# Long convolution and spectral mix on one core: earlier W reads, ten Z rooms, and the identity behind the last pair

## The chip, the cores and the metric

The kernel runs on one core of one Trainium2 chip. The metric is the time of one execution in device microseconds; lower is better. Engines are named as the profile names them: PE (matmuls), PEld (its weight loads), DVE, ACT, POOL and SP. POOL and SP also issue DMAs: POOL's go to the queue that the profile calls q0 software_dynamic, SP's to q1 hardware_dynamic. Both queues are served by the same 16 DMA engines.

## What is computed

`x` is 8 x 5696 x 128, `h` is 5696 x 128, and there are 64 modes with complex 128 x 128 matrices. Cut to what matters:

```python
L = 2 * S                                   # causal convolution along the sequence
y = irfft(rfft(x, L) * rfft(h, L), L)[:, :S]
X = rfft(y)[:, :64]                         # spectral mix of the first 64 modes
Yr = einsum(Xr, w_r) - einsum(Xi, w_i)
Yi = einsum(Xr, w_i) + einsum(Xi, w_r)
u = y + irfft(Yr + 1j * Yi, n=S)
out = u + relu(u @ w_ch)
```

## The kernel before

The eight batches go through in four pairs (`NP = 4`). The work has three parts.

*First transforms* (`a_tile`, 32 tiles per pair): a transform of the input over 89 rows, into the tile `As`.

*Frequency ticks* (`tick(g_, t)` for each pair `g_`, 23 pieces `s = 0 .. 22` and three ticks of lag): a second transform from `As` with the constants `M` into PSUM (`second`), ACT's copy of it to `Xs`, DVE's product with the transformed filter `Hs` (`products`, into `U`), two matmuls with `Wc`, and two evictions by ACT into a *Z room*, a 128 x 1024 tile. From the room PE reads the piece for the low modes (constants `G`, one tick later), and a DMA on SP's queue writes it to the scratch tensor `zscr` in HBM (512 rows of 512 bytes; half of that for piece 22). A room is free for its next piece when both have happened. Rooms 0 to 5 are called `Zs` in the profile, 6 to 9 `Zt`. Between two pairs the next pair's first transforms run (L700), and the pieces of w_r and w_i are rewritten to the scratch tensor `wscr`.

*The tail* (from L710): the mix of the 64 modes with `W` (2 x 64 matrices, read back from `wscr` into `W` in four DMAs of 1 MB), eviction of the result to `Y` (L780), eight transposes of `Y` on PE with the identity `Id` as moving operand (L785), eviction to `C`, and then 16 chunks of 16 sequence columns: each is read from `zscr` into `ZT0` to `ZT4` in turn (a DMA of 128 rows of 8 KB and one of 52 rows), transformed back with `S4a` and `S4b`, joined with the mix's part (`C`, `IBs`), evicted to `UT`, and multiplied by `w_ch` (`WI`); ACT's relu and DVE's addition make the output tile, which SP's queue writes out. A part of chunk 0's matmuls is done between the parts of the mix.

Each engine has one list of instructions, in the order in which the program adds them; `Recorder` adds the waits that reads and writes of named tokens require. `after=` adds a wait for all that wrote or read a token before. A DMA takes its semaphore from a ring, and waits for the ring's earlier user of that semaphore.

What the change touches:

- `NZS` (L230): the rooms per pair, 6, 10, 10 and 8. With 8 in the last pair, rooms 8 and 9 are not used in it; the tile `Y` and the identity lie in their memory (`r_off`, L274). `ZY` names the tokens of these two rooms, `ZX` those of rooms 6 and 7.
- the ring "z" of the writes to `zscr` (L293), with 8 semaphores.
- `early` (L529): what the last pair starts at which tick, on POOL's queue: the identity at 0, W's pieces at 1, 3, 6 and 8, `S4b` at 12, the clearing of `ZT0b` at 14, `ZT0` at 15, `S4a` at 16, and at 21 `IBs`, `ZT1` and `ZT2`. `pace` makes each wait for the tick's `U`.
- `SLACK` (L535): `ZT1` waits until the last pair's pieces 0 to 14 have landed in `zscr`. `ZT3` and `ZT4` follow after the loop (L711 to L714), all in POOL's one queue.
- `load_w` (L483): each piece waits for all writes of `wscr`; piece 0 also for all reads of the input tile `Xin`, in whose memory `W` lies.

Of the kernel before, what the change touches and what calls it, by code (L numbers as in the profile page):

```python
# [4 lines left out]
P = 128  # L5
# [118 lines left out]
def bass_long_conv_fft__then__afno_spectral_mix_kernel(nc, x, h, moe_w_r, moe_w_i, moe_w_ch, out):  # L124
# [8 lines left out]
    NP = B // 2  # L133
    KT = 4
    NT = (NK + KT - 1) // KT
# [15 lines left out]
    c, s = np.cos(th), np.sin(th)  # L151
# [35 lines left out]
    def const(name, a):  # L187
        return nc.inline_tensor(np.ascontiguousarray(a.astype(np.float16)), name=name)
# [3 lines left out]
    c_w = const("cW", np.concatenate([w1, w2, np.eye(P)], axis=1))  # L192
# [5 lines left out]
    zs = nc.dram_tensor("zscr", [NP * NK * P, 2 * D], F16, kind="Internal")  # L198
# [7 lines left out]
    def at(name, cols, dt, off):  # L206
        return nc.alloc_sbuf_tensor_at(name, [P, cols], dt, offset=off)

    def take(nbytes):
        off = (cur[0] + 31) // 32 * 32  # L210
        cur[0] = off + nbytes
        assert cur[0] <= end, (cur[0], end)
        return off
# [13 lines left out]
    g_sb = at("G", GW, F16, a_g)  # L227
    ah_sb = at("Ah", HW, F16, a_g)
    NU, NXS, NZ, NZX = 3, 2, 6, 10
    NZS = [NZ] + [NZX] * (NP - 2) + [8]  # L230
    NZL = NZS[-1]
    a_st = take((2 * NU + NXS + NZ) * 2048)
    h_in = at("Hin", J * D, F16, a_st)
    DH = D // 2
# [45 lines left out]
    id_sb = at("Id", P, F16, r_off[1])  # L280
# [8 lines left out]
    def pv(bank, off, dims, p0=0, n=P):  # L289
        return bass.AP(ps, p0 * 4096 + bank * 512 + off, [[4096, n]] + [list(d) for d in dims])  # L290

    R = Recorder(nc)
    for name, n in (("c", 16), ("x", 26), ("z", 8), ("w", 16), ("t", 10), ("s", 8), ("o", 12), ("p", 16), ("q", 10)):  # L293
        R.ring(name, n)

    def bank(i):
        return ("bank", i)
# [3 lines left out]
    def evac(dst, src, reads, writes, scale=None, eng=None, after=()):  # L301
        e = eng
        if e is None:
            turn[0] ^= 1
            e = "scalar" if turn[0] else "vector"
        if e == "scalar":
            if scale is None:
                R.add(e, lambda h_: h_.copy(dst, src), reads, writes, after=after)  # L308
            else:
                R.add(e, lambda h_: h_.activation(dst, src, COPY, scale=scale), reads, writes, after=after)  # L310
        elif scale is None:
            R.add(e, lambda h_: h_.tensor_copy(dst, src), reads, writes, after=after)  # L312
        else:
            R.add(e, lambda h_: h_.tensor_scalar_mul(dst, src, scale), reads, writes, after=after)  # L314

    def dma(eng, dst, src, ring, reads=(), writes=(), after=()):
        R.add(eng, lambda h_: h_.dma_start(dst, src), reads, writes, ring=ring, after=after)  # L317
# [6 lines left out]
    def once(key, toks):  # L324
        if key in first:
            return []
        first[key] = 1
        return list(toks)
# [3 lines left out]
    def turns(name, items):  # L332
        i = ring2.get(name, 0)
        ring2[name] = i + 1
        return items[i % len(items)]
# [87 lines left out]
    for j in range(16):  # L423
        t = turns("h", [0, 2, 4])
# [11 lines left out]
        if j % 2:  # L436
            i = j // 2 % 2 * XC + j // 4
# [45 lines left out]
    def load_w(i):  # L483
        w = 2 * M * D // 4
        dma("gpsimd", w_sb[:, i * w:(i + 1) * w], bass.AP(wd, i * w, [[2 * M * D, P], [1, w]]),
            "p", WD, [("w", i)] + (XIN if i == 0 else []), after=pace)
# [4 lines left out]
    M_ALL = [("m", i) for i in range(MP)]  # L491
    G_ALL = [("g", i) for i in range(NG)]
    WT = [("w", i) for i in range(4)]
    ZY = [("zs", i, b) for i in range(NZL, NZX) for b in range(2)]
    ZX = [("zs", i, b) for i in range(NZ, NZL) for b in range(2)]
    zt_old = [(AST, AST), (AST, AST), (H_ALL, H_ALL), (H_ALL, H_ALL), (M_ALL[3:6], G_ALL)]

    def load_zt(i, eng="sync", more=()):
        g_, c_ = divmod(i, J // ZB)
        for part, (p0, r0, n) in enumerate(((0, 0, P), (PB, P, RB))):  # L500
            old = list(once(("zt", i % NC, part), zt_old[i % NC][part])) + list(more) + pace
            dma(eng, bass.AP(zt[i % NC][part], p0 * ZP, [[ZP, n], [1, ZP]]),
                bass.AP(zs, (g_ * 2 * NK + r0) * J * 256 + c_ * ZB * 256, [[J * 256, n], [1, ZP]]),
                "q" if eng == "gpsimd" else "t", [("zd", g_, s_) for s_ in range(NT)], [("zt", i % NC, part)], after=old)

    def clear_zt(i):
        z32 = zt[i][1][0:PB, :].bitcast(U32)
        R.add("gpsimd", lambda e: e.memset(z32, 0), (), [("zt0", i)], after=list(zt_old[i][1]) + pace)

    def load_ib():  # L510
        dma("gpsimd", ib_sb[:, 0:SH], c_ib.ap(), "p", (), [("ib", 0)], after=M_ALL[0:2] + pace)
# [10 lines left out]
    def load_s4(part):  # L522
        n = PB + RB if part else P
        dma("gpsimd", s4_sb[part][0:n, 0:SH], bass.AP(c_s4, part * SH, [[2 * SH, n], [1, SH]]), "p", (),
            [("s4", part, 0)], after=pace + (AST if part else M_ALL[1:4]))

    V, A = "vector", "scalar"
    border = {NT - 1: [(0, 0, V)], NT: [(1, 2, V), (2, 0, V)], NT + 1: [(3, 2, A), (4, 0, V)], NT + 2: [(5, 2, V)]}
    early = {0: lambda: load_id(), 1: lambda: load_w(0), 3: lambda: load_w(1), 6: lambda: load_w(2), 8: lambda: load_w(3),  # L529
             12: lambda: load_s4(1), 16: lambda: load_s4(0),  # L530
             14: lambda: clear_zt(0),
             15: lambda: load_zt(0, "gpsimd"),
             NT - 2: lambda: (load_ib(), load_zt(1, "gpsimd", SLACK), load_zt(2, "gpsimd"), clear_zt(1), clear_zt(2))}
    pace = []
    SLACK = [("zd", NP - 1, s_) for s_ in range(NT - NZL)]  # L535

    def load_id():
        dma("gpsimd", id_sb[:, :], bass.AP(c_w, 2 * P, [[3 * P, P], [1, P]]), "p", (), [("id",)], after=ZY)

    def load_wi():  # L540
        dma("gpsimd", wi_sb[:, P:2 * P], bass.AP(c_w, 2 * P, [[3 * P, P], [1, P]]), "p", (), [("i16",)], after=M_ALL[5:6])
# [2 lines left out]
    def keep(n, b0):  # L544
        for i in range(n):
            mm(pv(b0 + i % 2, 0, [[1, 2 * NK]]), f1_sb[:, 0:P], f1_sb[:, :], True, True, [("f1",)], [bank(b0 + i % 2)])
# [66 lines left out]
    def zroom(g_, s_):  # L613
        return (s_ - 2 * NZ) % NZX if g_ == 0 and s_ >= 2 * NZ else s_ % NZS[g_]

# [69 lines left out]
            filter_tick((j - 11) // 3, [h_, h_ + 1])  # L685
    keep(16, turns("s", FOUR))
    for g_ in range(NP):
        for t in range(NT + LM):
            tick(g_, t)
            if g_ == 0 and t < 2:  # L690
                keep(8, 4)
            assert g_ + 1 < NP or not wp
            if g_ == NP - 1 and t in early:
                pace[:] = [("u", min(t, NT - 1) % NU)]
                early[t]()
        evac(bass.AP(xt, 2 * g_ * XTW + M, [[B * XTW, P], [XTW, 2], [1, P]]), pv(MB, 0, [[P, 2], [1, P]]),
             [bank(MB)], [("xt", g_)], 1.0 / 64, eng="scalar", after=[("ag", k) for k in range(NS + 2 * XN, NK)])
        evac(bass.AP(xt, 2 * g_ * XTW, [[B * XTW, P], [XTW, 2], [1, M]]), pv(MB, M, [[P, 2], [1, M]]),
             [bank(MB)], [("xtn", g_)], -1.0 / 64, eng="vector" if g_ + 1 == NP else "scalar", after=[("ag", k) for k in range(NS + 2 * XN, NK)])
        if g_ + 1 < NP:  # L700
            for j in range(6, 32):
                a_tile(j, [(4, 6, 0, 2)[(j - 7) % 4] if j > 6 else 0], "both" if j == 31 else V if j % 2 else A)
                if j == 31:
                    keep(8, 6)
                if wp and j % 2 == 1:
                    dst, src_, ring, tok = wp.pop(0)
                    dma("gpsimd", dst, src_, ring, (), [tok], after=[("as", j)])
# [71 lines left out]
    for hb in range(2):  # L779
        evac(bass.AP(y_sb, hb * 32 * B, [[2 * M * B, P], [B, 32], [M * B, 2], [1, B]]),  # L780
             pv(6 + hb, 0, [[2 * B, 32], [B, 2], [1, B]]), [bank(6 + hb)], [("y", hb)], eng="vector" if hb else "scalar",
             after=ZY)
    for b in range(B):
        bk = 6 + b // 4
        R.add("tensor", lambda e, b=b, bk=bk: e.transpose(  # L785
# [10 lines left out]
    o_cur = [0]  # L796
    o8_old = [H_ALL] * 2 + [U_ALL] + [G_ALL + ZX] * 2 + [WT] * 2
    o_old = [H_ALL] * 2 + [M_ALL[5:6], U_ALL + [("f1",)]]
# [49 lines left out]
    for g_ in range(NP):  # L848
        last = g_ == NP - 1
        order = [(c_, b) for b in range(2) for c_ in range(NCH)] if last else [(c_, b) for c_ in range(NCH) for b in range(2)]  # L850
        for n, (c_, b) in enumerate(order):
            i = NCH * g_ + c_
# [44 lines left out]
```

## Time and profile before

| | |
|---|---|
| median of 3 runs | 393.89 us (393.86 to 394.1) |
| the profiled execution | 392.87 us, of which span 390.6 us |
| PE busy | 364.1 us, 93% of the span |
| DVE, ACT, POOL busy | 301.9 us, 311.2 us, 85.6 us |
| DMA | 103.94 MB, mean 266 GB/s |
| ticks of the last pair | about 221 to 263 us |
| mix, transposes, first UT eviction | 264 to 273 us |
| chunks and output | to the end |

A profile line of a group gives line, engine, operation, tile written and tiles read, and a count. A wait line says who waited for whom, the total, how often, and the longest. The chain is the work that ended last, followed back from the end. A DMA's time to landing runs from its issue to the update of its semaphore. All times within the execution are counted from the span's start.

### The profile page before, as it was taken

What the parts mean: (1) busy time and instruction counts of PE and PEld (TensorE: products, weight loads), DVE (VectorE), ACT (ScalarE), POOL (GpSimd) and SP (SyncE); (2) the same over time, 40 slices, a digit from 0 to 9 for tenths busy, and PEclk for the clock granted to TensorE, in tenths of its full rate; (3) what the DMA queues carried; (4) which work ended last, traced back from release to release, by engine and by line L of the source; (5) the groups of instructions that cost most, each with busy time, mean ns of one, the idle gap of its engine ahead of it and who ended that gap; (6) DMA issues with size and microseconds to landing.
All of it is one profiled execution on the core that took longest, in us unless ns stands there. A gap on an engine that the chain in (4) does not pass through costs nothing.

```text
span 390.6 us, 12485 instructions
## 1 busy us (share of the span) xinstructions
PE 364.1 (93%) x5346; PEld 281.3 (72%) x5346; DVE 301.9 (77%) x346; ACT 311.2 (80%) x489; POOL 85.6 (22%) x134
## 2 busy tenths in 40 slices
PE   7799899998989999999989899989989999999992
PEld 7698766665866667856657666658878988988871
DVE  3369889987998998989998988754437767677784
ACT  8289689997989997899997899984447676777783
POOL 8600022210643210823213210319200000000000
PEclk9899999999999999999999999996999999999998
DMA  7998569998899995999995689999999999998766
GB/s 146 178 283 337 138 126 297 274 251 251 92 135 201 238 268 169 127 136 231 245 261 111 64 264 351 298 354 379 406 388 393 414 407 412 410 399 356 305 274 273
DMA packets 87090, 103.94 MB, mean 266 GB/s; under 512 B 22824, under 2 KB 72616, under 8 KB 83564
## 3 DMA queue, kind: packets, MB, share of 16 engines
q1 hardware_dynamic: 62523, 67.73, 49.7%
q0 software_dynamic: 24512, 35.43, 43.6%
q8 instruction: 42, 0.69, 0.7%
q14 instruction: 13, 0.10, 0.1%
HBM read 70.61 MB, written 51.12 MB: 312 GB/s over the span
## 4 chain that ended last, share of the span: by engine, by line
PE 63%; DMA 15%; DVE 8%; ACT 6%; issue 3%; POOL 3%; SPq 0%; POOLq 0%; DVEq 0%
PE ps L320 63%; DMA ZT4b<-zscr 4%; DMA zscr<-Zt 3%; DMA Hs<-Hs 3%; DMA Hin<-in_h_dram 3%; DMA Xt<-in_x_dram 2%; DVE As L314 2%; DVE U L599 2%; ACT As L310 2%; DVE U L607 1%; DVE Xin L361 1%; ACT UT L308 1%; ACT Zs L308 1%; DVE Hs L312 1%; ACT Xs L308 1%
## 5 line engine op out<-in xcount | busy, mean ns | idle before, releaser
L607 DVE TENSOR_TENSOR U<-Xs,Hs 128x2048 f16<-128x2048 f16 (+1 forms) x73 | 86.9, 1192 | 15.1 <-ACT Xs L308 11.0
L320 PE MATMUL ps<-U,Wc 128*128 128x512 f16 (+1 forms) x368 | 94.0, 376 | 1.3 <-DVE U L607 0.8
L308 ACT CAST Xs<-ps 128x1024 f16<-128x1024 f32 (+1 forms) x77 | 74.7, 974 | 11.9 <-PE ps L320 6.8
L308 ACT CAST Zs<-ps 128x512 f16<-128x512 f32 (+1 forms) x134 | 70.6, 595 | 2.7 <-PE ps L320 2.4
L832 DVE TENSOR_TENSOR O<-ps,R 128x512 f32<-128x512 f32 x81 | 52.5, 685 | 19.8 <-ACT R L831 12.5
L831 ACT ACTIVATE R<-ps 128x512 f32<-128x512 f32 x96 | 50.9, 572 | 16.3 <-PE ps L320 15.8
L314 DVE TENSOR_SCALAR As<-ps 128x720 f16<-128x720 f32 x70 | 57.7, 884 | 5.4 <-PE ps L320 4.8
L320 PE MATMUL ps<-F,Xin 128*128 128x180 f16 x512 | 53.7, 249 | 3.6 <-DVE Xin L361 2.3
L320 PE MATMUL ps<-As,M 64*128 64x128 f16 x1440 | 50.5, 217 | 3.5 <-DVE U L599 2.9
L320 PEld LDWEIGHTS ps<-F,Xin 128*128 128x128 f16 x512 | 44.4, 155 | 12.1 <-DVE Xin L361 2.8
L320 PE MATMUL ps<-WI,UT 128*128 128x256 f16 x360 | 51.8, 279 | 0.5 <-DVE O L832 0.4
L320 PEld LDWEIGHTS ps<-U,Wc 128*128 128x128 f16 x368 | 28.7, 97 | 30.3 <-ACT Zs L308 4.4
L310 ACT ACTIVATE As<-ps 128x720 f16<-128x720 f32 (+1 forms) x61 | 45.7, 770 | 5.7 <-PE ps L320 4.3
L317 POOL DMA_DIRECT2D Xt<-in_x_dram x48 | 26.0, 546 | 101.0 <-PE ps L320 97.1
L320 PEld LDWEIGHTS ps<-As,M 64*128 64x128 f16 x1440 | 40.6, 94 | 9.9 <-DVE U L599 3.6
L308 ACT CAST UT<-ps 128x712 f16<-128x712 f32 x40 | 30.0, 752 | 18.7 <-PE ps L320 17.7
L320 PEld LDWEIGHTS ps<-WI,UT 128*128 128x128 f16 x360 | 39.3, 152 | 4.2 <-issue 1.9
L320 PE MATMUL ps<-IBs,C 128*128 128x356 f16 x128 | 40.5, 326 | 0.6
L320 PEld LDWEIGHTS ps<-G,Zs 128*128 128x128 f16 x524 | 26.6, 96 | 14.9 <-ACT Zs L308 2.2
L607 DVE TENSOR_TENSOR U<-ps,Hs 128x2048 f16<-128x2048 f32 x15 | 34.3, 2283 | 0.0
L320 PE MATMUL ps<-G,Zs 128*128 128x128 f16 (+2 forms) x524 | 33.0, 192 | 0.1
L312 DVE CAST UT<-ps 128x712 f16<-128x712 f32 x24 | 21.4, 890 | 11.0 <-PE ps L320 11.0
(87 smaller groups left out, 509.8 us busy)
## 6 DMA issues: line engine op xcount, KB each, us to landing
out_dram<-O SPq DMA_DIRECT2D x39, 512.0 KB, 8.7
zscr<-Zs SPq DMA_DIRECT2D x64, 256.0 KB, 7.4
Xt<-in_x_dram POOLq DMA_DIRECT2D x24, 320.0 KB, 7.3
zscr<-Zt SPq DMA_DIRECT2D x24, 256.0 KB, 7.3
W<-wscr POOLq DMA_DIRECT2D x4, 1024.0 KB, 9.1
M<-cM POOLq DMA_DIRECT2D x5, 720.0 KB, 20.6
ZT0a<-zscr SPq DMA_DIRECT2D x3, 1024.0 KB, 13.1
Hs<-Hs SPq DMA_DIRECT2D x44, 64.0 KB, 6.3
```

What stands on the lines that cost most here:

```text
L308: R.add(e, lambda h_: h_.copy(dst, src), reads, writes, after=after)
L310: R.add(e, lambda h_: h_.activation(dst, src, COPY, scale=scale), reads, writes, after=after)
L312: R.add(e, lambda h_: h_.tensor_copy(dst, src), reads, writes, after=after)
L314: R.add(e, lambda h_: h_.tensor_scalar_mul(dst, src, scale), reads, writes, after=after)
L317: R.add(eng, lambda h_: h_.dma_start(dst, src), reads, writes, ring=ring, after=after)
L320: R.add("tensor", lambda h_: h_.matmul(o, l, r, start=st, stop=sp), reads, writes)
L361: R.add("vector", lambda e: e.tensor_copy(bass.AP(x_sb, i * XN * XS, [[XW, NQ], [XS, XN], [1, D]]), src), list(toks) + XZ, [("xin", i)])
L599: R.add("vector", lambda e, b=b, s_=s_: e.tensor_tensor(bass.AP(u_s[i], b * 512, [[2048, P], [1024, 2], [1, n * D]]), s_, hv, MULT), [tok, ...
L607: R.add("vector", lambda e: e.tensor_tensor(uv, src, hv, MULT), bk + [("h", t, 0), ("h", t, 1, 0), ("h", t, 1, J)], [("u", i)])
L831: R.add("scalar", lambda e: e.activation(rv, src_r, RELU), bk, [("r", i % NR)], after=once(("r", i % NR), G_ALL + XTT + [("y", 0), ("y", 1 ...
L832: R.add("vector", lambda e: e.tensor_tensor(ov, src_u, rv, ADD), bk + [("r", i % NR)], [key + (h_,)], after=once(key, old))
```

## The change

```diff
-    NZS = [NZ] + [NZX] * (NP - 2) + [8]
-    NZL = NZS[-1]
+    NZS = [NZ] + [NZX] * (NP - 1)
...
-    for name, n in (("c", 16), ("x", 26), ("z", 8), ("w", 16), ...
+    for name, n in (("c", 16), ("x", 26), ("z", 10), ("w", 16), ...
...
-    ZY = [("zs", i, b) for i in range(NZL, NZX) for b in range(2)]
-    ZX = [("zs", i, b) for i in range(NZ, NZL) for b in range(2)]
+    ZX = [("zs", i, b) for i in range(NZ, NZX) for b in range(2)]
...
-    early = {0: lambda: load_id(), 1: lambda: load_w(0), 3: lambda: load_w(1), 6: lambda: load_w(2), 8: lambda: load_w(3),
-             12: lambda: load_s4(1), 16: lambda: load_s4(0),
+    early = {3: lambda: load_w(2), 6: lambda: load_w(3), 10: lambda: load_s4(1), 16: lambda: load_s4(0),
              14: lambda: clear_zt(0),
              15: lambda: load_zt(0, "gpsimd"),
-             NT - 2: lambda: (load_ib(), load_zt(1, "gpsimd", SLACK), load_zt(2, "gpsimd"), clear_zt(1), clear_zt(2))}
+             18: lambda: load_ib(),
+             NT - 2: lambda: (load_zt(1, "gpsimd", SLACK), load_zt(2, "gpsimd"), clear_zt(1), clear_zt(2)),
+             NT + 2: lambda: load_id()}
     pace = []
-    SLACK = [("zd", NP - 1, s_) for s_ in range(NT - NZL)]
+    SLACK = [("zd", NP - 1, s_) for s_ in range(NT - 8)]
 
     def load_id():
-        dma("gpsimd", id_sb[:, :], bass.AP(c_w, 2 * P, [[3 * P, P], [1, P]]), "p", (), [("id",)], after=ZY)
+        dma("sync", id_sb[:, :], bass.AP(c_w, 2 * P, [[3 * P, P], [1, P]]), "c", (), [("id",)], after=ZX)
...
     for g_ in range(NP):
+        if g_ == NP - 1:
+            load_w(0)
+            load_w(1)
         for t in range(NT + LM):
...
         evac(bass.AP(y_sb, hb * 32 * B, [[2 * M * B, P], [B, 32], [M * B, 2], [1, B]]),
              pv(6 + hb, 0, [[2 * B, 32], [B, 2], [1, B]]), [bank(6 + hb)], [("y", hb)], eng="vector" if hb else "scalar",
-             after=ZY)
+             after=ZX)
```

`NT` is 23. `SLACK` covers the same pieces 0 to 14 as before. `ZX` now names rooms 6 to 9, all of which the last pair uses: the identity's load and both evictions to `Y` wait for what was last read from them. The identity's load is SP's last issue of the pair, behind the write of piece 22. `W`'s pieces 0 and 1 are issued by POOL ahead of the last pair's first tick, without a pace. Apart from the two rooms more, the instructions on PE, ACT and DVE and their order stay as they were; the lines behind the edit in `NZS` move up by one and those behind the two new calls down.

More of the change, by code (lines that the diff above doesn't have):

```diff
@@ L292, in bass_long_conv_fft__then__afno_spectral_mix_kernel @@
     R = Recorder(nc)
-    for name, n in (("c", 16), ("x", 26), ("z", 8), ("w", 16), ("t", 10), ("s", 8), ("o", 12), ("p", 16), ("q", 10)):
+    for name, n in (("c", 16), ("x", 26), ("z", 10), ("w", 16), ("t", 10), ("s", 8), ("o", 12), ("p", 16), ("q", 10)):
         R.ring(name, n)
```

## The prediction

> **What bounds the kernel now.** I read the page first: PE is busy 93% of the span, so a gain or a loss is time in which PE waits. Next the waits by pair between 215 and 300 us, where the last pair runs and the tail begins:
>
> ```profile
> POOL ZT1a L317 <- DMA zscr<-Zt: 2.4, 1, 2.4
> ACT Zt L308 <- DMA zscr<-Zt: 1.0, 1, 1.0
> PE ps L320 <- DMA ZT4b<-zscr: 1.8, 1, 1.8
> ```
>
> Columns: who waited for whom, total, times, longest. ACT stands 1.0 us before the last Z piece (s = 22) because room Zt0 still holds s = 14, whose write to zscr has not landed. PE stands 1.8 us before chunk 4. The chain that ended last ties the two (start, us, what):
>
> ```profile
> 250.16 11.91 DMA zscr<-Zt
> ...
> 262.59 0.53 POOL ZT1a L317
> ...
> 273.48 15.12 DMA ZT4b<-zscr
> 288.59 0.05 issue
> 288.64 11.36 PE ps L320 x163
> ```
>
> Piece 14's write, issued at 250.16, takes 11.91 us. ZT1a waits for it (SLACK), everything behind ZT1a on POOL's queue follows, and ZT4b lands at 288.59. Between 288 and 391 us the waits name PE, ACT and DVE among each other and no DMA but that ZT4b, so the tail is paced by the engines: what PE loses before it is added to the end.
>
> Third, the identity's tile, the eight transposes that need it, and its load:
>
> ```profile
> L785 PE MATMUL ps<-Id,Y x8: 302/311/311, 269.8 to 270.6; 128*128 128x128 f16 x8
> L317 POOL DMA_DIRECT2D Id<-cW x1: 569/569/569, 216.4 to 216.4; - x1
> ```
>
> The load is issued 53 us ahead. The transposes stand in PE's one queue: while they wait, all that follows waits.
>
> Fourth, the queue to which the load moves. SP's last issue of the pair and its time to landing, and both DMA queues between 268 and 272 us (packets, MB, share):
>
> ```profile
> 264.31 1.89 SPq L317 DMA_DIRECT2D zscr<-Zt  x1
> ```
> ```profile
> zscr<-Zt SPq DMA_DIRECT2D x1, 128.0 KB, 20.1
> ```
> ```profile
> q0 software_dynamic: 236, 1.43, 88.3%
> q1 hardware_dynamic: 263, 0.13, 11.0%
> ```
>
> The smallest write of all takes 20.1 us, from 264.31 to 284.4. The last fence shows why: POOL's queue (q0, rows of 8 KB) and SP's (q1, rows of 512 B) get one packet each in turn, so SP moves an eleventh of the bytes as long as POOL's ZT loads last.
>
> **W pieces 0 and 1 ahead of the pair.** In the trace they are issued at 225.28 and 228.43. They need the last first transforms (PE is through them at 219.9) and the last write of wscr, which lands at 220.7 (issued at 215.71, 5.0 us). So they go at about 221. No PE wait is named after W: piece 3, the last, is issued at 236.75, takes 9.2 us, and is first used at 264.4. Directly this earns 0. Indirectly it lets 2 MB go while DMA is idle: from 215 to 225 us it moves 60 GB/s and nothing after 221. The start is 4.5 us earlier, and piece 14 (5 us behind its queue now) meets less: it may land between 254 and 262 in place of 262.07. Then ZT1a is held by the pace of tick 21 alone, which let the IB load go at 259.62 in this trace: ZT1a goes between 259.7 and 262.6, a gain of 0 to 2.9 us for the ZT stream. S4b's and IB's earlier ticks move the same bytes; nothing waits for either in the trace: 0. But IB, 128 packets, leaves a stretch (259 to 264 us) in which SP sent 2160 packets and POOL 123; in its new place, about 254.4 (three ticks of 1.75 us ahead), it runs right behind S4a and leaves the writes of pieces 15 to 19 later than now.
>
> **Ten rooms and a ring of ten.** Piece 22 takes room 2 of piece 12, whose write has landed by 253.0. ACT's 1.0 us goes, if PE's next need is not later anyway. The old ring of eight is not named in any wait: 0.
>
> **The identity behind SP's queue.** One DMA of 32 KB, 128 packets of 256 B, so 8 on each of 16 engines; SP's issue costs some 0.4 us of an idle sequencer. It is issued after piece 22's write (so not before 263), waits until the writes of pieces 16 to 19 (rooms Zt0 to Zt3) have landed, and its packets stand behind those of pieces 20, 21 and 22: 32+32+16 per engine. Landings of SP's queue are in order throughout the trace (273.5, 280.4, 284.4 for these three). Both Y evictions get the same wait for pieces 16 to 19, and the transposes need Y as well.
>
> The price: the ZT stream has 45 packets of 8 KB per engine (four chunks of 128+52 rows, over 16) and 16 small ones of WI. At 1.43 MB in 4 us (268 to 272) the stream's 5.9 MB take 16.5 us, or 0.27 us for each of an engine's 61 packets. In that time SP gets about as many turns, 61, fewer than the 80 packets ahead of the identity. So the identity lands no sooner than POOL's stream runs dry. The nearest row says the same: piece 22 landed 21.8 us after ZT1a's issue. With ZT1a at 259.7 to 262.6 this is 281.5 to 284.4; the identity's own 8 packets and its wait for piece 19, later than now through IB, add 0.5 to 3. I take 285.0, near the upper end because of that wait; bounds 281 to 288. Nothing covers it: the 16 matmuls and the eviction that precede the transposes are done by 269.8, and ACT, DVE and POOL have nothing that feeds PE.
>
> **The sum.** Transposes at 285.0 in place of 269.84: +15.2. From there PE needs the 17 us of work it has now before chunk 4; that chunk has long landed by 302, so its wait of 1.8 goes. ACT's 1.0 us lies ahead of the new stall and earns 0; without the stall it would count. Sum +13.4 us. The profiled execution is 390.6 us of span and 392.87 in all; it becomes 404.0 and 406.3. The median of the runs is 393.89, 1.0 above, so 407.3.
>
> The clock: granted 0.82 in 263 to 270 and 0.56 in 270 to 275, 1.00 before and after, so the transposes already meet a slow PE. [...] My sum takes the cost as equal on both sides, since the trace shows 4.5 us at the low rate after 269.84 now; bounds -0.6 and +1.2.
>
> **Rivals.**
> 1. *SP's queue is served in bigger bites.* If SP gets several packets per turn, pieces 20 to 22 and the identity pass during the first two chunks: ZT2b landed 15 us after ZT1a's issue (277.6), so with ZT1a at 259.7 to 262.6 the identity lands at 274.7 to 277.6, say 276: +6.2-1.8, so 398.3. For it: 2160 packets of SP in 5 us when POOL has little. Against: 236 against 263 with both full. [...]
> 2. *The identity is in time.* If the earlier W empties the queues so far that pieces 16 to 22 land by 266, the identity is there at about 268.8, and both old waits go: -1.0-1.8, so 391.1. It decides below a landing of 271.6 (269.84 plus 1.8 given back); past that the change costs. For it: the queues hold up to 1.6 MB less by 250 (4.5 us at 0.36 MB/us). Against: pieces 20 to 22 are evicted between 259.3 and 262 however empty the queues are, ZT1a follows by 262.6 at the latest, and in that company their writes took 11.4, 17.6 and 20.1 us.
> 3. *It doesn't reach the end.* The identity lands at about 271.6, so that the stall only takes the place of the waits given back: 393.9. Against: the same three writes; and a longer stall isn't made up later, since PE is busy 39.6 of 40 us from 310 to 350.
>
> **Chances.** Forecast 0.82, rival 1 0.10, rival 2 0.06, rival 3 0.02. A measurement tells this kernel from no change at about 0.2%, 0.8 us. Faster 0.06, same 0.02, slower 0.92. Range: identity at 281 to 288 and the clock's bounds give 402.7 to 411.5; I widen it to 401 to 412 towards rival 1.
>
> **What would show it.** Right: one PE wait of 12 to 18 us before L787 (the transposes' new line), ended by the DMA of Id; Id issued on SP after 263 and landing near 285; W's first two loads at about 221; no ACT wait for room Zt0; no PE wait before chunk 4; the tail from the transposes to the end as long as now less 1.8 us. Wrong: Id landing before 272, a PE wait there under 2 us, or a tail that shortens by more than the clock's 1.2 us.

## The result and the profile after

| | before | changed |
|---|---|---|
| median of 6 runs | 393.14 us (388.19 to 394.1) | 404.66 us (402.09 to 407.3) |
| ratio to the kernel before | 1 | 1.034, 95% interval 1.029 to 1.039 |
| profiled execution: span | 390.6 us | 400.0 us |
| transposes begin | 269.84 us | 283.64 us |
| from there to the span's end | 120.8 us | 116.4 us |

The change costs 3.4%. The ratios here and below leave out runs over 1.5% above the fastest of their kernel (three of ten in e1, one of ten in e8, two and three of twelve in e3 and e7, three of six in e11), so they can differ from the quotients of the medians. The profiled execution of the changed kernel, 402.09 us in all, is the fastest of its six.

The four longest waits of the changed kernel between 215 and 310 us, in the same columns as before, among them all those on a DMA; L787 is the transposes' new line:

```profile
ACT Y L307 <- DMA zscr<-Zt: 16.7, 1, 16.7
PEld ps L787 <- issue: 16.2, 1, 16.2
PE ps L787 <- DMA Id<-cW: 16.0, 1, 16.0
DVE Y L311 <- DMA zscr<-Zt: 15.8, 1, 15.8
```

Both old waits (ACT for room Zt0, PE for ZT4b) are gone. In their place PE stands 16.0 us once. The chain that ended last shows what leads there:

```profile
258.94 0.40 ACT Zs L307
259.33 21.79 DMA zscr<-Zt
281.12 0.02 issue
281.14 2.36 DMA Id<-cW
283.50 0.14 issue
283.64 1.04 PE ps L787 x8
```

The write of room Zt3 (piece 19), 256 KB, takes 21.79 us from its issue. Its landing releases two things at once: the evictions to Y, and SP, which then issues the identity. The identity lands 2.36 us later, at 283.50. From the view of its tile:

```profile
L316 SPq DMA_DIRECT2D Id<-cW x1: 332/332/332, 281.1 to 281.1; - x1
...
DMA to landing us min/median/max: 2.4/2.4/2.4
```

The room is not the only thing that held it. SP's write of piece 22, the last ahead of the identity, with its time to landing:

```profile
273.71 4.32 SPq L316 DMA_DIRECT2D zscr<-Zs  x1
281.14 0.33 SPq L316 DMA_DIRECT2D Id<-cW  x1
```
```profile
zscr<-Zs SPq DMA_DIRECT2D x1, 128.0 KB, 9.6
```

SP was through with issuing this write at 278.03, and it landed at 283.33, 0.2 us before the identity.

The windows of the changed kernel show the hole (columns: stretch, length, busy time of PE, PEld, DVE, ACT and POOL, granted clock, DMA share, GB/s):

```profile
263.00:270.00 7.00, 4.65 (x137) 4.45 (x133) 2.39 (x1) 1.52 (x1) 7.00 (x9) 0.76 1.03 398
270.00:283.60 13.60, 0.00 (x0) 0.00 (x0) 0.69 (x1) 0.59 (x1) 1.68 (x1) 0.50 0.78 294
283.60:287.00 3.40, 3.36 (x23) 2.51 (x24) 2.09 (x3) 1.09 (x2) 0.00 (x0) 0.50 0.00 0
287.00:300.00 13.00, 13.00 (x239) 11.45 (x238) 4.50 (x5) 6.23 (x10) 0.00 (x0) 1.00 0.73 262
```

PE does nothing from 270 to 283.6, and after 283.6 the DMA engines stand too: all five chunks are there, and the next loads need PE's first. On POOL's side, the forecast head start came:

```profile
258.99 0.53 POOL L316 DMA_DIRECT2D ZT1a<-zscr  x1 [4.79 <-PE ps L319]
```

ZT1a is issued at 258.99, not 262.59, released by its tick and no longer by piece 14 (the chain before had it). W's first pieces are issued at 220.77 and 221.31, and piece 14's write takes 3.8 us (248.96 to 252.72) where it took 11.91.

### The profile page after: what moved, and what is told of

It reads as the page before. It is cut to its first block, busy times and chain, and to the rows that moved or that the text cites. A ratio compares the mean times of both kernels' runs of the same rounds, so it can differ in the third digit from the quotient of the medians.

```text
span 400.0 us, 12468 instructions
## 1 busy us (share of the span) xinstructions
PE 361.3 (90%) x5346; PEld 279.0 (70%) x5346; DVE 303.4 (76%) x346; ACT 310.7 (78%) x489; POOL 83.3 (21%) x133
## 4 chain that ended last, share of the span: by engine, by line
PE 67%; DMA 14%; DVE 7%; ACT 6%; POOL 3%; issue 2%; DVEq 0%; POOLq 0%
PE ps L319 67%; DMA zscr<-Zt 5%; DMA Xr<-in_x_dram 4%; DMA Xt<-in_x_dram 4%; DVE As L313 2%; DVE U L598 2%; POOL Xr L316 2%; ACT As L309 2%; ACT R L833 1%; DVE Xin L360 1%; ACT Xs L307 1%; ACT UT L307 1%; DVE Hs L311 1%; ACT Zt L307 1%; POOL Hin L316 1%
## 5 line engine op out<-in xcount | busy, mean ns | idle before, releaser
L307 ACT CAST Zs<-ps 128x512 f16<-128x512 f32 (+1 forms) x128 | 67.0, 594 | 2.2 <-PE ps L319 2.2
L319 PEld LDWEIGHTS ps<-G,Zs 128*128 128x128 f16 x496 | 25.3, 96 | 14.0 <-ACT Zs L307 2.0
L307 ACT CAST Zt<-ps 128x512 f16<-128x512 f32 x56 | 30.4, 615 | 1.6 <-PE ps L319 1.6
L319 PE MATMUL ps<-G,Zs 128*128 128x2 f16 (+2 forms) x496 | 31.3, 192 | 0.1
```

What stands on the lines that cost most here:

```text
L319: R.add("tensor", lambda h_: h_.matmul(o, l, r, start=st, stop=sp), reads, writes)
```

## The experiments

Three theories of the 16 us that PE stands. **A, the room:** the write that leaves room Zt3 last; Y and the identity lie in the memory of rooms 8 and 9 (Zt2, Zt3) and wait for rooms 6 to 9. **B, the queue:** the identity stands behind SP's writes of pieces 20 to 22, which crawl beside POOL's ZT loads. **C:** Y's wait alone. All ratios are to the kernel before on the same chip.

### e1_id: the identity elsewhere and early

```diff
-    id_sb = at("Id", P, F16, r_off[1])
+    id_sb = at("Id", P, F16, a_xt + 8192)
...
-             NT + 2: lambda: load_id()}
...
-        dma("sync", id_sb[:, :], ...
+        dma("gpsimd", id_sb[:, :], ...
...
+            load_id()
             load_w(0)
```

> The changed kernel, but the identity lies in 256 free bytes behind Xin and is loaded by POOL ahead of the last pair; Y stays in the memory of rooms 8 and 9. Theory A (the room's write: the stall lasts until piece 19's write lands, at 281.1 in the changed kernel, for Y needs that memory): Y is evicted at 281 as before, the transposes begin at about 282 in place of 283.6, and the time falls by only 1 to 2 us, to some 403. Theory B (the queue: the identity stands behind SP's writes of pieces 20 to 22): the stall is gone, the transposes begin at about 269, and the time is about 391.

Measured: 399.23 us beside 391.57 for the kernel before, ratio 1.013 (1.009 to 1.018), with single runs from 394.1 to 405.4. In the profiled execution, the fastest of them, the chain reads:

```profile
258.96 15.14 DMA zscr<-Zt
274.09 0.03 ACTq L115
274.12 0.04 issue
274.16 0.59 ACT Y L308
274.75 0.21 issue
274.96 1.05 PE ps L788 x8
```

Neither number was met. The room's wait is there without the identity, but piece 19 landed at 274.1, not 281.1, and PE stood 6.8 us. Here piece 19 was issued 0.6 us ahead of ZT1a (258.96 against 259.55); in the changed kernel 0.3 us behind it (259.33 against 258.99). In e2, e3 and e5 below it was ahead as well, and piece 19 landed at 272.9 to 275.8. That order may be what spreads e1's runs over 11 us; this is not shown, since only one execution of each kernel has a profile.

### e2_y: Y elsewhere, the identity as in the change

```diff
-    y_sb = at("Y", 2 * B * M, F16, r_off[0])
+    y_sb = at("Y", 2 * B * M, F16, a_st)
...
-             after=ZX)
+             after=[("u", 0)])
```

> The changed kernel, but Y lies in the memory of U0, which is free when the mix ends; the identity stays behind the last pair in the memory of room 9. Theory A (the room's write) and theory B (the queue) both: the identity is issued at about 281 after piece 19's landing and lands at about 283.5; Y is evicted at about 265 to 268; the time stays at 404 to 405. Theory C (Y's wait alone makes the stall, and the identity's is hidden): the transposes begin at about 269 and the time is about 391.

Measured: 403.74 us, ratio 1.030 (1.024 to 1.035). C falls. The time is as A and B expected, but not by A's path:

```profile
257.42 15.50 DMA zscr<-Zt
272.94 9.44 DMA Id<-cW
282.51 1.05 PE ps L787 x8
```

Piece 19 landed at 272.9, 8 us earlier than in the changed kernel, and the identity was issued at once, yet it took 9.44 us in place of 2.36 and landed at 282.4. The write of piece 22 landed at 282.2. So with the room free 8 us earlier, the queue alone holds the identity until nearly the same time.

### e4_ib21 and e6_rooms_only: parts of the change undone around the identity

e4 puts the load of IBs back to tick 21. e6 puts all ticks back and keeps ten rooms, the identity behind the pair, and Y after rooms 6 to 9:

```diff
-    early = {3: lambda: load_w(2), 6: lambda: load_w(3), 10: lambda: load_s4(1), 16: lambda: load_s4(0),
+    early = {1: lambda: load_w(0), 3: lambda: load_w(1), 6: lambda: load_w(2), 8: lambda: load_w(3),
+             12: lambda: load_s4(1), 16: lambda: load_s4(0),
...
-             18: lambda: load_ib(),
-             NT - 2: lambda: (load_zt(1, "gpsimd", SLACK), ...
+             NT - 2: lambda: (load_ib(), load_zt(1, "gpsimd", SLACK), ...
...
-        if g_ == NP - 1:
-            load_w(0)
-            load_w(1)
```

> The changed kernel with the load of IBs back at tick 21. If the earlier IBs is what keeps pieces 16 to 19 on SP's queue until POOL's stream is over: these land by 266 to 271, Y is evicted by 271, the identity is issued then, stands behind pieces 20 to 22, and lands at about 281 to 284: the time stays within 2 us of the changed kernel, 403 to 406, and the wait is of the queue in place of the room. If the ZT stream alone does it: piece 19 lands at 279 to 282 as in the changed kernel, and the time is the same too. Rival: a small transfer is served between POOL's rows, the identity lands 2 to 4 us after its issue, at about 273, and the time is about 395.

> The changed kernel with W, S4b and IBs back at their old ticks; ten rooms, the identity behind the last pair, Y after rooms 6 to 9. If the identity's place behind pieces 20 to 22 makes the stall: piece 14 lands at about 262, ZT1a goes at 262.6, piece 19 lands at 267 to 270, the identity is issued then and lands with piece 22 at 284 to 287; PE stands 15 to 17 us and the time is 404 to 407. If the earlier ticks make it: the identity lands within 5 us of its issue, and the time is 393 to 396.

Measured: e4 404.32 us, ratio 1.032 (1.026 to 1.037); e6 404.91 us, ratio 1.034 (1.029 to 1.039). The chain of e4, then of e6:

```profile
260.70 6.03 DMA zscr<-Zt
266.75 18.86 DMA Id<-cW
285.74 1.05 PE ps L786 x8
```

```profile
259.98 11.41 DMA zscr<-Zt
271.40 14.91 DMA Id<-cW
286.45 1.04 PE ps L784 x8
```

With IBs at its old tick piece 19 lands at 266.7 (271.4 in e6, where the other ticks are old too), so the earlier IBs made the room's write slower. The time doesn't change: the identity, issued 14 us earlier than in the changed kernel, takes 18.86 us and lands at 285.6, 0.2 us after piece 22 (285.4). In e6 it lands at 286.3, again 0.2 us after piece 22. So the rooms with the identity's new place carry the whole loss, and W's earlier read none of it.

### e8_act: the identity on a queue of its own

```diff
-             NT + 2: lambda: load_id()}
...
-        dma("sync", id_sb[:, :], ...
+        dma("scalar", id_sb[:, :], ...
...
+    load_id()
     for hb in range(2):
         evac(bass.AP(y_sb, ...
```

This is e4 with the load issued by ACT ahead of Y's eviction.

> The changed kernel with IBs back at tick 21 and the identity's load issued by ACT, just ahead of the eviction of Y, so that it has a DMA queue to itself. If the place behind SP's pieces 20 to 22 is what makes the identity late: issued at 267 to 268, it passes beside POOL's and SP's rows in 8 turns and lands at 270 to 273, PE stands 1 to 4 us, and the time is 391 to 395. If the DMA engines are simply full until the ZT stream ends: it lands at 280 or later, and the time is 402 to 406.

Measured: 394.63 us, ratio 1.008 (1.004 to 1.012); nine runs lie between 391.9 and 397.2, and one took 403.4, for which no profile shows the reason. The chain:

```profile
258.65 5.96 DMA zscr<-Zt
264.63 8.18 DMA Id<-cW
272.90 1.05 PE ps L786 x8
```

The same 32 KB against the same ZT stream: 8.18 us in place of 18.86, and PE stands 4.8 us in place of 15.8. The DMA engines weren't too full for the identity; its place in SP's line was the cost. This tells B from all that is left of A.

### e3_id_y and e7_shift: neither wait

e3 joins the edits of e1 and e2 (R's first use then waits for rooms 6 to 9 itself). e7 keeps the memory of Y and Id, and lets go of it earlier:

```diff
-        return ... else s_ % NZS[g_]
+        return ... else (s_ - 8) % NZX if g_ == NP - 1 and s_ >= 18 else s_ % NZS[g_]
...
+    ZY = [("zs", i, b) for i in range(8, NZX) for b in range(2)]
...
+    early = {..., 10: lambda: load_s4(1), 13: lambda: load_id(), 16: lambda: load_s4(0),
...
-             NT + 2: lambda: load_id()}
```

with `ZY` in place of `ZX` for the identity and Y.

> The changed kernel with both the identity and Y in other memory, so that neither waits for a room. Theory A and B: no wait of PE ahead of the transposes over 1 us, no wait of ACT for a room, ZT4b landed before chunk 4: the 1.0 us at the last piece and most of the 1.8 us before chunk 4 of the kernel before are gone, 390 to 391.5 beside 393.1. Rival: the tail is paced by DMA at its end, so that what PE gains before it is lost again at the last outputs: 393.

> The changed kernel, but pieces 18 to 22 of the last pair go to rooms 0 to 4, so that rooms 8 and 9 end with pieces 8 and 9; identity and Y wait for these two alone, and the identity is issued at tick 13 on SP's queue. Room and queue theory: no stall ahead of the transposes, no wait for a room (room 4's piece 14 lands by 255), 389 to 391 beside 391.6, as the kernel with both tiles moved. Rival: SP's queue, held at tick 13 until piece 9 has landed, delays the writes behind it, and ZT1a by SLACK: 391 to 393.

Measured: e3 390.54 us, ratio 0.996 (0.993 to 1.000); e7 390.42 us, ratio 0.995 (0.992 to 0.998). In both the stall is gone, and with the rest of the change the kernel is a little faster than before, though e3's interval all but reaches 1. e7's identity lands in 1.6 us at tick 13. That there would be no wait for a room didn't hold: DVE stands 2.2 us for one of the last writes before an eviction to UT at 287.16, with no wait of PE behind it. e7's profiled execution, at 392.1 us one of the slower of its runs, shows a new wait in the tail (335 to 375 us):

```profile
DVE O L834 <- DMA out_dram<-O: 3.0, 1, 3.0
...
PE ps L319 <- DVE O L834: 2.0, 1, 2.0
```

### e5_w_only, e9_before and e10_w_again: the new ticks alone

e5 and e10 are the kernel before with the new ticks: eight rooms, the identity early on POOL's queue.

> The kernel before with the new ticks alone: W's pieces 0 and 1 ahead of the last pair, pieces 2 and 3 at ticks 3 and 6, S4b at 10, IBs at 18; eight rooms, the identity early on POOL's queue, Y after rooms 8 and 9. If the backlog of DMAs is what held piece 14's write in the kernel before: it lands at 252 to 255, ACT no longer waits for a room, ZT1a goes at about 259.5, ZT4b is there before chunk 4, and the time falls by 1 to 2.8 us, to 389 to 390.5 beside 391.6. Rival: rooms and ring are needed for it, ACT's wait stays, and the time is within 0.5 us of before.

> The kernel before once more, unchanged, for a second profile of it beside the next run. If the two waits of the first profile are a property of the kernel: ACT waits about 1 us for a room at the last piece and PE 1 to 2 us before chunk 4, and output writes between 335 and 375 us take at most 14 us to land. If they were of that execution: at most one of them is seen, under 0.5 us.

> The kernel with the new ticks alone, once more, on the same chip as the kernel before. If the tail's DMAs take back what the earlier front earns: neither of the two old waits, output writes between 335 and 375 us landing later than in the kernel before, with DVE or PE waiting 1 to 5 us for one of them, and a ratio of 0.997 to 1.003. If the earlier result was the spread of the runs: no such wait, and a ratio of 0.993 to 0.996.

Measured: e5 391.38 us, ratio 1.000 (0.997 to 1.003); e9 392.71 us, 1.001 (0.997 to 1.005); e10 391.67 us, 1.000 (0.996 to 1.003). e5's expectation fell in the time and held in the profile, where none of PE, DVE and ACT waits for a DMA anywhere after 215 us. The second profile of the kernel before has the two waits of the first:

```profile
PE ps L320 <- DMA ZT4b<-zscr: 1.9, 1, 1.9
...
ACT Zt L308 <- DMA zscr<-Zt: 0.9, 1, 0.9
```

So they belong to the kernel, and e10's profile has neither. It has two others, after 310 us, the longer one under the 1 to 5 us that were expected:

```profile
DVE O L835 <- DMA out_dram<-O: 0.8, 1, 0.8
PEld ps L320 <- DMA ZT0b<-zscr: 0.6, 1, 0.6
```

Its output writes between 335 and 370 us take up to 16.0 us to land, against 12.0 us in e9 and 13.5 in the first profile of the kernel before. But the span of e10's profiled execution is still 3.3 us under e9's (388.5 and 391.8; e9's is the slowest of its twelve runs), while the medians are 1.0 us apart, and e5 and e10 equal the kernel before by ratio.

### e11_before_half and e12_w_half: the tail with half its output

```diff
-            dst = bass.AP(out.tensor, ..., [[NW * D, P], [1, w_]])
-            src = ob[:, 0:w_]
+            dst = bass.AP(out.tensor, ..., [[NW * D, P], [1, w_ // 2]])
+            src = ob[:, 0:w_ // 2]
```

Both leave out half of the output; e12 has the new ticks of e5 besides.

> The kernel before, with every full output tile written out by half only (each row's first half; the other half of the output is left out), to take the tail's DMA load away. The reference point for the next run. If the tail of the kernel before is paced by its engines: within 1 us of before but for the last writes, 390 to 392. If it is paced by DMA: below 389.

> The kernel with the new ticks alone, with every full output tile written out by half only (the other half of the output is left out). If the tail's DMAs take back what the two removed waits earn: here the gain shows in the time too, 2 to 3.3 us below the kernel before with half its output. If something else does: within 0.8 us of it.

Measured: e11 388.92 us, ratio 0.979 (0.974 to 0.985); e12 387.63 us, ratio 0.983 (0.978 to 0.988). Half the output is worth about 2% to the kernel before by the ratio, and 1.3% by the medians (388.92 beside 394.07), just past the expected mark for DMA. e11's one profile, of one of its slower runs (391.91 us), puts the gain at the end: from the last matmul to the span's end it takes 4.0 us, where the two profiles of the kernel before have 7.3 and 5.7. Between the 17th eviction to UT and the last matmul it takes 93.3 us in place of 93.7. So that DMA paces the tail ahead of its last writes isn't shown. Between the two kernels the medians say 1.3 us and the ratios the opposite, with intervals that overlap; neither number of e12 was met. It doesn't settle where the new ticks' gain goes.

## Why the prediction was right, step by step

**Sign, place and most of the size.** It said one PE wait of about 15 us at the transposes, ended by the identity's landing at 285.0; it was 16.0 us and 283.50. The steps behind it held: W at about 221 (220.77), ZT1a released by its tick alone (258.99, 0.7 us ahead of the forecast stretch), no wait of ACT for room Zt0, none before chunk 4.

**The reason for the landing.** "The identity lands no sooner than POOL's stream runs dry" is what e2, e4 and e6 show, and the changed kernel with them:

| | identity issued | ZT4b landed | piece 22 landed | identity landed |
|---|---|---|---|---|
| changed | 281.14 | 282.12 | 283.33 | 283.50 |
| e2 | 272.94 | 280.98 | 282.20 | 282.38 |
| e4 | 266.75 | 285.21 | 285.43 | 285.60 |
| e6 | 271.40 | 285.76 | 286.11 | 286.31 |

Whenever it is issued, the identity lands 0.2 us after piece 22. In the changed kernel's own profile the chain names the room, since piece 19's landing at 281.12 let the identity go; but the queue ahead of it was only empty at 283.33. The prediction had the room's wait as an addition of 0.5 to 3 us; in truth the two overlap, and either is enough for a stall. Alone the room made 6.8 us in e1's profile, the queue all of it in e4. That IBs' earlier tick delays pieces 15 to 19 was right (266.7 without it), and cost nothing that the time shows.

The good number is in part luck. Piece 22 landed 24.3 us after ZT1a's issue, not 21.8 as in the kernel before, and ZT1a went earlier than forecast; the two misses offset each other. The count of turns was also misread: of POOL's 236 packets, 61 are records of 4 bytes in the trace, so 175 rows of 8 KB (1.43 MB) stand against 259 of 512 B, one and a half of SP's for one of POOL's. At that rate the 88 packets in SP's line take about as long as POOL's 61, not longer, so the turns alone didn't put the identity behind the stream.

**The sum was 2.6 us too high in the median** (407.3 against 404.66). Against the kernel before, the forecast was +13.4 us and the medians of the same series say +11.5; the profiled spans say +9.4. In the profiles the transposes moved by 13.8 in place of 15.2. The tail's term was mis-sized: from the transposes to the end it shortened by 4.4 us, not 1.8. That is past the limit that the prediction set itself, even if its 1.2 us are read as on top of the 1.8; as they are written, the two lines contradict each other. Of the 4.4 us, 2.0 lie in the stretch that held the wait before chunk 4 (between the 13th and the 17th eviction to UT, 5.9 us before and 3.9 after), 0.5 ahead of it, 0.2 behind it, and 1.7 at the end, from the last matmul to the span's end: 7.3 us before and 5.6 after. The second profile of the kernel before has 5.7 there, so the end varies by as much from one execution to the next, and against that profile the tail is 3.1 us shorter.

**The clock.** The sum took the clock's cost as equal on both sides. Its bounds of -0.6 and +1.2 us, which went into the range, are shown by no run; what the runs showed in their place is this. The granted clock was 0.50 for the whole idle stretch and until 287.06, 3.4 us after the transposes began; before, it stayed at 0.50 for 4.5 us from there. The 1.1 us less at 0.50 are 0.55 us of work, an estimate from the granted 0.50 and 1.00. That fits the 0.5 us gained ahead of the 13th eviction: the fourth eviction to UT comes 4.51 us after the transposes in the changed kernel and 5.00 in the kernel before. The fall to 0.50 came at 266.58, ahead of the idle stretch, and PE was busy for all of the 3.4 us before it (3.40 us busy from 263.18 to 266.58); why it came there stays open.

**Rivals.** *Bigger bites* for SP: out as it was priced, by the four landings behind piece 22. Beside them, e8's 8.2 us in place of e4's 18.86 shows that the identity's 128 packets of 256 B cost far less when nothing of their own queue is ahead. *In time:* the condition wasn't met, but e3 and e7 meet it, at 0.996 and 0.995 of the kernel before; the prediction's 391.1 is 0.993 of its 393.89. *No reach:* out.

**The two old waits.** The sum gave 1.8 us for ZT4b and would have given 1.0 for the room. In the changed kernel's profile the first came back in full. Without the stall the profiles say the same: the tail takes 117.9 us in e5 and 117.0 in e10, and 120.8 and 119.4 in the two profiles of the kernel before. The medians don't: e5 and e10 gain nothing that can be measured, e3 and e7 gain 0.4 to 0.5%, and the intervals overlap. One profile of each kernel says little about 2 us, since the start of the transposes alone differs by 2.5 us between the two of the kernel before (269.84 and 272.37). A tail that runs close to its DMAs (e7's 3.0 us, e10's 0.8 us for an output buffer) fits, but what becomes of the gain wasn't shown.

## What to carry to other kernels

The small load here cost what stood ahead of it in its own queue (18.86 us to landing behind SP's writes in e4, 8.18 us on ACT's queue in e8, 1.6 us at tick 13 in e7): look up the slowest landing there before moving a load to its end, and give a load that gates an engine a queue without bulk writes, or issue it before them. A tile that borrows the memory of a ring of rooms inherits the landing of that ring's last transfer (piece 19's, 281.12 in the changed kernel); if the last pieces are sent to other rooms, the memory is free early, in e7 at no cost that the time shows. Waits that a profile names need not be worth their length: taking away 1.8 and 1.0 us here moved no ratio (e5 and e10 are at 1.000).

## What was not expected of the hardware

DVE's scaling of S4a (2759 elements of fp16) took 0.93 us in the kernel before and 3.18 us in the changed one; POOL's two clearings stand beside the second:

```profile
264.18 0.93 DVE L520 TENSOR_SCALAR S4a<-S4a,SG 128x2759 f16<-128x2759 f16 x1
```

```profile
262.21 3.18 DVE L518 TENSOR_SCALAR S4a<-S4a,SG 128x2759 f16<-128x2759 f16 x1
```

```profile
261.08 1.82 POOL L506 MEMSET ZT1b<- 32x2048 uint32 x1
262.83 1.82 POOL L506 MEMSET ZT2b<- 32x2048 uint32 x1
```

It ends at 265.39, 0.74 us after POOL's second clearing (264.65), as if DVE had stood until POOL was done. With the clearings moved ahead with ZT1, they meet S4a's scaling in place of IBs', which goes from 2.10 to 0.93 us. DVE's own first eviction to UT then comes 2.3 us after the transposes in place of 3.4, but the fourth eviction doesn't gain by it: e1 has the short scaling too, and is at 5.04 us where the kernel before is at 5.00. The rows of the kernel before agree with that reading: there IBs' scaling (271.27 to 273.37) ends 0.74 us after the clearing of ZT3b (270.81 to 272.63). Why DVE stands was not shown.
